# Seven products of quarter sums for the first expert matrix, weights fetched in four parts, tokens read back from DRAM

## The chip, the cores and the metric

The kernel runs on one core of a Trainium2 chip. The metric is the device time of one execution in microseconds (us). Five engines work side by side: TensorE (PE in the profile; PEld is its weight load), VectorE (DVE), ScalarE (ACT), GpSimd (POOL) and SyncE (SP), whose queue issues nearly all DMAs here.

## The reference

```python
attn_out = attention(q, k, v)             # 4 batches, 8 heads, 576 tokens, head 64, two sparse masks
x = attn_out as (2304, 512)
# first mixture, dense: every token goes through all 8 experts
P = exp(x @ w_gate - max), scaled 8 times by rows and by columns
out = 0
for e in range(8):
    h = np.maximum(x @ w1[e], 0.0)        # w1[e]: 512 x 1024
    ye = h @ w2[e]                        # w2[e]: 1024 x 512
    out += P[:, e:e + 1] * ye
# second mixture: each token goes to one expert, at most 288 tokens an expert
out2[mask] = relu(out[mask] @ w1b[e]) @ w2b[e]
```

## The kernel before

Every matrix is held as two f16 parts, a high one and a low one, and a product of two matrices is three f16 products (high·high, high·low, low·high) that accumulate in one PSUM bank. The span has three stages: attention, with expert 0 in blocks of 256 tokens beside it (to some 370 us); the other experts of the first mixture, one after another (to some 1640 us); and the routing and the experts of the second mixture.

Experts are counted from 0 here. Expert e of the first mixture works on blocks of 512 tokens (four, and one of 256). For one block `l1` (L729) makes 8 slices of 128 rows of h. A slice is 4 x 3 = 12 matmuls in one PSUM bank; ACT then writes the high part `hh` with its ReLU (L732), and DVE the low part `hl` (L733). `l2` (L747) makes the block's tiles of 128 tokens: 8 x 3 = 24 matmuls of 512 columns in a bank, which DVE adds, scaled, to the sum `acc` (L779, called done below). `blocks` issues l1 of block b+1 ahead of l2 of block b, so there are two sets of hh and hl, and TensorE always has a block whose inputs are ready. PSUM has 2 banks under the tag `bank`, 3 under `l1` and 3 under `l2`.

Work on weights runs beside this, in steps of a generator that `weave` spreads over the blocks by counts written out by hand, each step issued on its engine behind the last instruction of the block work (`behind`). `w_fetch` (L567) loads one raw f32 matrix of 2 MB into the one buffer `raw`; `w_scale` finds its largest value (four DVE reductions, L588, a POOL reduction over partitions, L594, and a few small DVE operations); `w_split` writes the high part on ACT (L612) and the low part on DVE (L616), four pieces of 1024 columns. `w_prep` does this for both matrices of the next expert, `m2_prep` for both matrices of an expert of the second mixture, whose parts go to DRAM (`wd`). `late_w` multiplies the last expert's second matrix by the second gate (128 DVE products of 256 columns, L929), and `logits` multiplies tokens by the second gate on DVE (L904).

All of these DMAs stand in SP's queue in the order in which a scheduler puts them, and an issue that waits for a buffer holds those behind it.

Of the kernel before, what the change touches and what calls it, by code (L numbers as in the profile page):

```python
# [39 lines left out]
EPAD = 3  # L40
# [21 lines left out]
DIRECT = 14, 15  # L62

# [28 lines left out]
class Kernel:  # L92
# [468 lines left out]

    def w_src(self, name, e, j):
        return self.a[f"{name}_w{j + 1}"][e].rearrange("(c p) f -> p c f", p=128)

    def w_fetch(self, name, e, j):
        r = self.ws_pool.tile([128, 4096], F32, name="raw").rearrange("p (c f) -> p c f", c=(DC, FC)[j])
        self.nc.sync.dma_start(out=r, in_=self.w_src(name, e, j))  # L567
        return r

    def loading(self):  # L570

        yield from self.pad(LOAD)

# [8 lines left out]
    def w_scale(self, r, j, inv, early):  # L582
# [12 lines left out]
        if early:  # L595
            yield
# [7 lines left out]
    def w_split(self, raw, s, hi, lo, mode="a"):  # L604
# [12 lines left out]
        else:  # L617
            nc.gpsimd.tensor_tensor(lo, raw, hi, op=OP.subtract)

# [7 lines left out]
    def w_prep(self, e, w, raw=None, js=(0, 1)):  # L627

        for j in js:
# [14 lines left out]
            for k in range(nw):  # L644
# [3 lines left out]
                yield  # L648

# [69 lines left out]
    def l1(self, w, t0, nb, h):  # L719

        nc = self.nc
        hh, hl = h
        for f in range(FC):
# [3 lines left out]
            for d in range(DC):  # L727
                for l, r in ((w[0], self.xh), (w[0], self.xl), (w[1], self.xh)):
                    nc.tensor.matmul(ps, l[:, d, fs], r[:, d, t0:t0 + nb], start=k == 0, stop=k == 3 * DC - 1)  # L729
                    k += 1  # L730
# [6 lines left out]
    def l2(self, w, t0, nb, h, done, fine=False):  # L737
# [3 lines left out]
        for j in range(nb // 128):  # L741
# [3 lines left out]
            for f in range(FC):  # L745
# [3 lines left out]
                if f < FC - 1 and (self.fine or fine and f % 2):  # L749
                    yield 0  # L750
            with self.tc.high_priority(offset=AHEAD):
# [10 lines left out]
            yield 2  # L762
# [30 lines left out]
    def blocks(self, jobs, pool, nb, fine=False):  # L793

        last = None
        for job in self.chain(jobs, (None,)):
            if job:
                e, w, t0, n, done = job
                h = [pool.tile([128, FC, nb], F16, name=x) for x in ("hh", "hl")]
# [45 lines left out]
    def m2_prep(self, e):  # L845

        nc = self.nc
        for j in range(2):
# [5 lines left out]
            for k in range(2):  # L854
# [3 lines left out]
                for p in (slice(0, 1024), slice(1024, 2048)):  # L858
                    self.w_split(rf[:, q][:, p], s, hi[:, p], lo[:, p])
                    yield  # L860
# [707 lines left out]
```

## Time and profile before

| what | value |
|---|---|
| time, median of 3 runs | 1994.17 us (1992.65 to 1994.55) |
| the profiled execution's own time | 2000.29 us |
| its span in the trace | 1998.4 us |
| TensorE busy | 1934.8 us, 97% |
| VectorE busy | 1159.3 us, 58% |
| ScalarE, GpSimd busy | 527.7 us (26%), 186.8 us (9%) |
| DMA | 172.05 MB, mean 86 GB/s |
| mean granted TensorE clock | 0.975 of full speed |

TensorE's busy time counts overlapping instructions once, so it shows how little of the span it stood without a matmul; how fast matmuls follow each other is read from the chain of work and the timeline.

### The profile page before, as it was taken

Reading aid. Unit: us, or ns where it says so; the run is one execution under the profiler, and the core shown is the slowest. Engines: PE = TensorE matmul, PEld = TensorE weight load, DVE = VectorE, ACT = ScalarE, POOL = GpSimd, SP = SyncE. Lnnn points to the kernel's source line nnn. Section 1 sums busy time; section 2 is a strip of 40 time slices with the busy share of each in tenths; the row PEclk is TensorE's granted clock in tenths of the full one; section 3 lists DMA queues with packets and bytes.
Section 4 is the critical chain, followed back from the end, with each engine's and each line's share of the span. In section 5 each row is a group of like instructions: output and inputs, shape, how many; then the busy total and the mean of one; then the engine's idle time right before and its main releaser. Section 6 shows DMA issues by size and latency. Waiting matters only on the chain.

```text
span 1998.4 us, 30818 instructions
## 1 busy us (share of the span) xinstructions
PE 1934.8 (97%) x12796; PEld 1101.8 (55%) x12796; DVE 1159.3 (58%) x2934; ACT 527.7 (26%) x1053; POOL 186.8 (9%) x272
## 2 busy tenths in 40 slices
PE   8899999999999999999999999999999999998997
PEld 7778777444544454454445444545454444666776
DVE  7687767465536554764555366434854788655530
ACT  4455543132123222111222133121201110222222
POOL 1423400000000000000000000000000002232231
PEclk9689999999999999999999999999999999998999
DMA  8412103014322441111134224321100003344360
GB/s 208 65 27 62 37 3 108 19 66 152 122 83 93 160 140 71 43 43 43 43 127 169 85 84 140 114 85 43 43 1 11 22 22 118 118 151 163 121 216 24
DMA packets 112252, 172.05 MB, mean 86 GB/s; under 512 B 65616, under 2 KB 70224, under 8 KB 107888
## 3 DMA queue, kind: packets, MB, share of 16 engines
q1 hardware_dynamic: 104432, 127.08, 19.7%
q0 software_dynamic: 7680, 43.01, 6.0%
q8 instruction: 100, 1.64, 0.3%
q14 instruction: 40, 0.33, 0.1%
HBM read 126.53 MB, written 43.54 MB: 85 GB/s over the span
## 4 chain that ended last, share of the span: by engine, by line
PE 75%; DVE 11%; DMA 6%; issue 4%; ACT 1%; POOL 1%; SPq 1%; another core or an unknown queue 0%; ACTq 0%; POOLq 0%; DVEq 0%
PE l L729 30%; PE l L747 30%; DMA raw<-in_moe_w_dram 5%; PE mm L1356 3%; PE mm L1384 3%; DVE wmx L588 3%; PE pcnt L1025 1%; DVE hl L733 1%; DVE m2l L616 1%; DVE w1l L616 1%; DVE w2l L616 1%; PE pt L282 1%; SPq L195 1%; PE ptp L414 1%; DMA wd<-m2l 1%
## 5 line engine op out<-in xcount | busy, mean ns | idle before, releaser
L729 PE MATMUL l<-xh,w1h 128*128 128x512 f16 (+1 forms) x1408 | 482.7, 343 | 12.7 <-DVE wmx L592 7.6
L729 PE MATMUL l<-xl,w1h 128*128 128x512 f16 (+1 forms) x1408 | 482.5, 343 | 0.0
L729 PE MATMUL l<-xh,w1l 128*128 128x512 f16 (+1 forms) x1408 | 482.4, 343 | 0.0
L747 PE MATMUL l<-w2h,hh 128*128 128x512 f16 x1152 | 437.7, 380 | 0.0
L747 PE MATMUL l<-w2l,hh 128*128 128x512 f16 x1152 | 437.2, 380 | 0.0
L747 PE MATMUL l<-w2h,hl 128*128 128x512 f16 x1152 | 437.2, 379 | 0.0
L729 PEld LDWEIGHTS <-w1h 128*128 128x128 f16 x2816 | 275.7, 99 | 241.2 <-issue 14.9
L732 ACT ACTIVATE hh<-l 128x512 f16<-128x512 f32 (+1 forms) x352 | 180.7, 517 | 765.8 <-PE l L729 765.3
L747 PEld LDWEIGHTS <-hh 128*128 128x128 f16 x2304 | 222.1, 98 | 258.3 <-issue 2.7
L733 DVE SCALAR_TENSOR_TENSOR hl<-l,hh 128x512 f16<-128x512 f32 (+1 forms) x352 | 206.4, 591 | 236.8 <-ACT hh L732 236.7
L779 DVE SCALAR_TENSOR_TENSOR acc<-l,pe,acc 128x512 f32<-128x512 f32 x126 | 94.2, 748 | 196.3 <-PE l L747 196.3
L729 PEld LDWEIGHTS <-w1l 128*128 128x128 f16 x1408 | 139.0, 99 | 112.8
L747 PEld LDWEIGHTS <-hl 128*128 128x128 f16 x1152 | 112.8, 98 | 136.3 <-issue 0.8
L588 DVE TENSOR_REDUCE wmx<-raw 128x1 f32<-128x1024 f32 x120 | 141.1, 1210 | 66.2 <-DMA raw<-in_moe_w_dram 66.2
L612 ACT ACTIVATE m2h<-raw,wscale 128x1024 f16<-128x1024 f32 x64 | 70.4, 1140 | 190.8 <-DVE iw L601 86.9
L616 DVE SCALAR_TENSOR_TENSOR m2l<-raw,wscale,m2h 128x1024 f16<-128x1024 f32 x64 | 80.1, 1281 | 46.0 <-DMA wd<-m2l 28.6
L594 POOL PARTITION_ALL_REDUCE wall<-wmx x32 | 11.2, 350 | 975.5 <-DVE wmx L592 975.5
L904 DVE SCALAR_TENSOR_TENSOR junk<-acc,raw 128x512 f32<-128x512 f32 x144 | 99.0, 688 | 3.4 <-DMA raw<-gt 1.5
L1361 DVE SCALAR_TENSOR_TENSOR h2l<-mm,h2h 128x288 f16<-128x288 f32 x64 | 28.6, 452 | 58.2 <-ACT h2h L1360 52.6
L929 DVE SCALAR_TENSOR_TENSOR junk<-raw 128x256 f32<-128x256 f32 x128 | 54.1, 423 | 11.7 <-DMA raw<-in_moe_w_dram 8.1
L612 ACT ACTIVATE w2h<-raw,wscale 128x1024 f16<-128x1024 f32 x28 | 30.1, 1137 | 93.0 <-DVE wscale L119 93.0
L325 ACT ACTIVATE sm<-sm,mx 72x72 f32<-72x72 f32 (+1 forms) x168 | 49.0, 371 | 1.3 <-DVE mx L317 1.1
(379 smaller groups left out, 2110.3 us busy)
## 6 DMA issues: line engine op xcount, KB each, us to landing
raw<-in_moe_w_dram SPq DMA_DIRECT2D x30, 2048.0 KB
wd<-m2h SPq DMA_DIRECT2D x32, 512.0 KB
wd<-m2l SPq DMA_DIRECT2D x32, 512.0 KB
q<-in_q_dram SPq DMA_DIRECT2D x32, 144.0 KB
k<-in_k_dram SPq DMA_DIRECT2D x32, 144.0 KB
acc<-in_moe_w_dram SPq DMA_DIRECT2D x2, 2048.0 KB
raw<-gt SPq DMA_DIRECT2D x2, 1024.0 KB
raw<-in_moe_w_dram SPq DMA_DIRECT2D x2, 1024.0 KB
```

Of the source, the lines that this page charges most:

```text
L588: nc.vector.tensor_reduce(mx[:, k:k + 1], r[:, k * n:k * n + n], axis=AX.XY, op=OP.max, apply_absolute_value=True)
L612: nc.scalar.activation(hi, raw, AF.Copy, scale=s1)
L616: nc.vector.scalar_tensor_tensor(lo, raw, s, hi, op0=OP.mult, op1=OP.subtract)
L729: nc.tensor.matmul(ps, l[:, d, fs], r[:, d, t0:t0 + nb], start=k == 0, stop=k == 3 * DC - 1)
L732: self.last = [nc.scalar.activation(hh[:, f, :nb], ps, AF.Relu).ins, nc.vector.scalar_tensor_tensor(hl[:, f, :nb], ps, 0.0, hh[:, f, :nb], ...
L733: nc.vector.scalar_tensor_tensor(hl[:, f, :nb], ps, 0.0, hh[:, f, :nb], op0=OP.max, op1=OP.subtract).ins]
L747: nc.tensor.matmul(ps, l[:, f, js], r[:, f], start=k == 0, stop=k == 3 * FC - 1)
L779: self.last = [nc.vector.scalar_tensor_tensor(a, ps, pe[:, c:c + 1], a, op0=OP.mult, op1=OP.add).ins]
L904: self.nc.vector.scalar_tensor_tensor(junk, self.acc[:, c], 1.0, self.wgb[:, e], op0=OP.mult, op1=OP.mult, accum_out=self.lg[:, c, e:e + 1])
L929: nc.vector.scalar_tensor_tensor(junk[:, :n], w[:, c], 1.0, g[:, e], op0=OP.mult, op1=OP.mult, accum_out=part[:, i, c, e:e + 1])
L1356: nc.tensor.matmul(ps, l[:, d, fs], xg[:, r], start=k == 0, stop=k == 3 * DC - 1)
L1384: nc.tensor.matmul(ps, l[:, f, dsl], r[:, f], start=k == 0, stop=k == 3 * FC - 1)
```

## The change

1. For experts 2 to 6 the first matrix and the tokens are cut in quarters, and the four quarters of h are made from seven products of sums of quarters in place of eight products. A block is 768 tokens (two halves of `PAIR` = 384), three blocks an expert. `group(g)` makes two slices of 128 rows of h (g and g+4) for the block: seven banks of 6 matmuls of 384 columns, which DVE, ACT and POOL add up in f32 in SBUF (`c1`, `c2`, `u2`, `m5`), and then ReLU and split on ACT and DVE. Four groups make a block's h; there is one set of hh and hl, in the space of the tokens `xh` and `xl`, and l2 of a block follows its groups at once.
2. The sums of quarters of the tokens are made in expert 1's stage (`x_sums`) and kept in DRAM (`xv`), beside a copy of the tokens (`xw`); each block loads its seven (393 KB each) into a ring of nine slots (`x_load`). The last expert reads tokens back from `xw` (`x_back`).
3. The sums of quarters of a first matrix (`w_sums1`) are made in the last l2 of the expert before.
4. A raw matrix is fetched by four DMAs, and split in pieces of 512 columns, with the low part one piece behind the high one (`splits`).
5. Expert 1 goes in blocks of 256 tokens. PSUM is 1 bank for `bank`, 5 for `l1` and 2 for `l2` until the last expert's end. `late_w` is made in two halves, in the stages of experts 1 and 3; half of the late logits move to expert 6's last block.

```diff
+LOAD2 = 14
...
-M2_AT = {1: (0, 1), 2: (2, 3), 3: (), 4: (4, 5), 5: (6, 7)}
+M2_AT = {2: (0, 1), 3: (2,), 4: (3, 4), 5: (5, 6), 6: (7,)}
+SIDE = {1: 24 + 27 + 46 + 19, 2: 170, 3: 140, 4: 170, 5: 170, 6: 130}
...
+PAIR = 384
+NBLK = N // (2 * PAIR)
+RING = 9
+
+W11, W12, W22, WS1, WS2, WS3, WS4 = range(7)
+X11, X21, X22, XT1, XT2, XT3, XT4 = range(7)
+PRODUCTS = (W11, X11), (WS2, XT2), (WS1, XT1), (WS3, XT3), (W12, X21), (WS4, X22), (W22, XT4)
+F_ORDER = [f + h * FC // 2 for f in range(FC // 2) for h in range(2)]
+BLOCK = 4 * 7 + 6 * 4
+HB = {"m5": 1, "u2": 1, "c1": 2, "c2": 1}
...
+    def x_sums(self, n, tiles):
+
+        nc = self.nc
+        g = nc.vector.tensor_tensor
+        a, b = (t[:, 0:PAIR] for t in tiles[:2])
+        outs = [t.bitcast(F16)[:, 0:2 * PAIR].rearrange("p (k t) -> p k t", k=2) for t in tiles[2:]]
+        t = n * 2 * PAIR
+
+        def out(v, c, s):
+            o = outs[v % 2]
+            nc.scalar.activation(o[:, 0], s, AF.Copy)
+            g(o[:, 1], s, o[:, 0], op=OP.subtract)
+            nc.sync.dma_start(out=self.xv[v, n, :, :, c], in_=o)
+        for c in range(2):
+            q = {k: (self.xh[:, d, t + o:t + o + PAIR], self.xl[:, d, t + o:t + o + PAIR])
+                 for k, d, o in ((11, c, 0), (12, c, PAIR), (21, c + 2, 0), (22, c + 2, PAIR))}
+            for v, l, r in ((XT1, 12, 11), (XT3, 22, 12)):
+                g(a, q[l][0], q[r][0], op=OP.subtract)
+                g(b, q[l][1], q[r][1], op=OP.subtract)
+                g(a, a, b, op=OP.add)
+                out(v, c, a)
+                yield
+                if v == XT1:
+                    g(b, q[22][0], a, op=OP.subtract)
+                    g(b, b, q[22][1], op=OP.add)
+                    out(XT2, c, b)
+                    yield
+                    g(a, b, q[21][0], op=OP.subtract)
+                    g(a, a, q[21][1], op=OP.subtract)
+                    out(XT4, c, a)
+                    yield
+
+    def x_load(self, n):
+
+        self.xb = {}
+        for _, v in PRODUCTS:
+            self.xb[v] = self.xr[self.xn % RING]
+            self.xn += 1
+            self.nc.sync.dma_start(out=self.xb[v], in_=self.xv[v, n])
...
+    def x_back(self, blocks):
+
+        for t, n in blocks:
+            for k, x in enumerate(self.xs.get(t, [x[:, :, t:t + n] for x in (self.xh, self.xl)])):
...
     def w_fetch(self, name, e, j):
-        r = self.ws_pool.tile([128, 4096], F32, name="raw").rearrange("p (c f) -> p c f", c=(DC, FC)[j])
-        self.nc.sync.dma_start(out=r, in_=self.w_src(name, e, j))
+
+        c = (DC, FC)[j]
+        r = self.raw.rearrange("p (c f) -> p c f", c=c)
+        src = self.w_src(name, e, j)
+        for k in range(0, c, c // 4):
+            self.nc.sync.dma_start(out=r[:, k:k + c // 4], in_=src[:, k:k + c // 4])
         return r
 
...
+    def splits(self, parts, s):
+
+        nc = self.nc
+        low = None
+        for raw, hi, lo in parts:
+            nc.scalar.activation(hi, raw, AF.Copy, scale=s)
+            if low:
+                nc.vector.scalar_tensor_tensor(low[2], low[0], s, low[1], op0=OP.mult, op1=OP.subtract)
+            low = raw, hi, lo
+            yield
+        nc.vector.scalar_tensor_tensor(low[2], low[0], s, low[1], op0=OP.mult, op1=OP.subtract)
...
+    def w_sums1(self):
+
+        nc = self.nc
+        g = nc.vector.tensor_tensor
+        H = FC // 2 * 128
+        r, s = self.wr, self.w1sc
+        n = H // 2
+        late = []
+        for k in range(2):
+            f = [slice(h * H + k * n, h * H + k * n + n) for h in range(2)]
+            a11, a12, a21, a22 = r[:, 0:2, f[0]], r[:, 2:4, f[0]], r[:, 0:2, f[1]], r[:, 2:4, f[1]]
+            t = self.wt[k]
+            o = slice(k * n, k * n + n)
+
+            def out(v, x, sc=s):
+                hi, lo = self.w1s[:, v, 0, :, o], self.w1s[:, v, 1, :, o]
+                nc.scalar.activation(hi, x, AF.Copy, scale=sc)
+                for l in late:
+                    nc.vector.scalar_tensor_tensor(*l, op0=OP.mult, op1=OP.subtract)
+                late[:] = [(lo, x, sc, hi)]
+            g(t, a21, a22, op=OP.add)
+            out(WS1, t)
+            yield
+            out(W11, a11)
+            g(a21, a11, a21, op=OP.subtract)
+            yield
+            out(WS3, a21)
+            g(t, t, a11, op=OP.subtract)
+            yield
+            out(WS2, t)
+            yield
+            out(W12, a12)
+            g(t, a12, t, op=OP.subtract)
+            yield
+            out(W22, a22, self.w1ns)
+            yield
+            out(WS4, t)
+            yield
+        for l in late:
+            nc.vector.scalar_tensor_tensor(*l, op0=OP.mult, op1=OP.subtract)
+        yield
...
+    def group(self, g):
+
+        nc = self.nc
+        hh, hl = self.hb
+        H = FC // 2
+        gs = slice(g * 128, g * 128 + 128)
+        a, b = slice(0, PAIR), slice(PAIR, 2 * PAIR)
+        tile = lambda name, n=1: self.hp.tile([128, n * PAIR], F32, name=name, bufs=HB[name])
+        v, add = nc.vector.tensor_tensor, nc.gpsimd.tensor_tensor
+        m5, u2, c1, c2 = tile("m5"), tile("u2"), tile("c1", 2), tile("c2", 2)
+
+        def split(f, c, t):
+            nc.scalar.activation(hh[:, f, t], c[:, t], AF.Relu)
+            todo.append(lambda: nc.vector.scalar_tensor_tensor(hl[:, f, t], c[:, t], 0.0, hh[:, f, t], op0=OP.max,
+                                                               op1=OP.subtract))
+        todo = []
+        for k, (w, x) in enumerate(PRODUCTS):
+            ps = self.bank("l1", "l1")[:, :PAIR]
+            n = 0
+            for c in range(2):
+                for l, r in ((0, 0), (0, 1), (1, 0)):
+                    nc.tensor.matmul(ps, self.w1s[:, w, l, c, gs], self.xb[x][:, r, c], start=n == 0, stop=n == 5)
+                    n += 1
+            now, todo = todo, []
+            with self.tc.high_priority(offset=AHEAD):
+                if k == 0:
+                    nc.scalar.activation(c1[:, a], ps, AF.Copy)
+                elif k == 1:
+                    v(u2, ps, c1[:, a], op=OP.add)
+                elif k == 2:
+                    nc.scalar.activation(m5, ps, AF.Copy)
+                    add(c1[:, b], u2, m5, op=OP.add)
+                elif k == 3:
+                    v(c2[:, a], ps, u2, op=OP.add)
+                    add(c2[:, b], c2[:, a], m5, op=OP.add)
+                elif k == 4:
+                    v(c1[:, a], ps, c1[:, a], op=OP.add)
+                    split(H + g, c2, b)
+                    split(g, c1, a)
+                elif k == 5:
+                    v(c1[:, b], ps, c1[:, b], op=OP.add)
+                    split(g, c1, b)
+                else:
+                    v(c2[:, a], ps, c2[:, a], op=OP.add)
+                    split(H + g, c2, a)
+                for f in now + (todo if k == 6 else []):
+                    self.last = [f().ins]
+            yield int(k in (0, 2))
+
+    def expert(self, e, order, first=None):
+
+        done = self.moe_done(e)
+        w2 = self.w2[e % 2]
+        for i, n in enumerate(order):
+            for g in range(FC // 2):
+                yield from self.group(g)
+            nxt = order[i + 1] if i + 1 < len(order) else first
+            if nxt is not None:
+                self.x_load(nxt)
+            else:
+                self.x_back(((2048, 256), (0, 512)))
+            yield from self.l2((None, None) + tuple(w2), n * 2 * PAIR, 2 * PAIR, self.hb, done, False,
+                               (3, 4, 5, 0, 1, 2))
...
+        self.banks = {"bank": 1, "l1": 5, "l2": 2}
...
+        for e in range(2, E - 1):
+            blk = self.expert(e, orders[e], orders[e + 1][0] if e + 2 < E else None)
+            side = [self.w_prep2(e + 1, self.w2[(e + 1) % 2])] + [self.m2_prep(k) for k in M2_AT[e]]
             if e == LATE_W:
-                side.append(self.late_w())
-                n += 65 + 2 * LOAD
-            self.weave((self.take(blk, 46 + 2 * (e > 1)), 55 if e == 1 else 58), (self.behind(self.chain(*side)), n))
-        self.weave((self.take(blk, 10), 10))
-        self.weave((self.take(blk, 24), 24), (self.behind(self.w_prep(E - 1, wts[1])), PIECES))
-        self.wgb = self.gate_bcast(self.ws_pool.tile([128, 4096], F32, name="raw"), 0, DM)
-        self.weave((self.take(blk, 22), 28), (self.behind(self.chain(*(self.logits(c) for c in LATE))), 4 * len(LATE)))
+                side.append(self.late_w(1))
+            if e == E - 2:
+                side.append(gates())
+            side.append(self.w_prep1(e + 1))
+            if e == E - 2:
+                side += [self.logits(c) for c in LATE[4:]]
+                for t, n, o in ((2048, 256, 0), (0, 512, 1024)):
+                    self.xs[t] = [x[:, o:o + DC * n].rearrange("p (d t) -> p d t", d=DC) for x in wf]
+            self.weave((self.take(blk, 2 * BLOCK + 4 * 7), 72), (self.behind(self.chain(*side)), SIDE[e]))
+            if e < E - 2:
+                self.weave((blk, 24), (self.behind(self.w_sums1()), 15))
+        fs = [slice(k, k + 512) for k in (0, 512)]
+        side = [self.splits([(self.wr[:, d, f], wts[1][0][:, d, f], wts[1][1][:, d, f]) for d in range(DC) for f in fs],
+                            self.w1sc)] + [self.logits(c) for c in LATE[:4]]
+        side = self.behind(self.chain(*side))
+        self.weave((blk, 24), (side, 20))
+        self.x_back(((t, 512) for t in (512, 1024, 1536)))
+        hs.close()
+        hb = hs.enter_context(tc.tile_pool(name="hb2", bufs=1, side="right"))
+        tail = w1s[:, 2 * DC * F:].rearrange("p (f t) -> p f t", t=512)
```

Three places of the order in which instructions stand.

VectorE in expert 3's stage before, in a block's l1 (`hl` is the low part of h, `m2l` that of a matrix of the second mixture):

```order
L601 TENSOR_TENSOR iw_66<-iw_66,wscale_i 128x1
L733 SCALAR_TENSOR_TENSOR hl<-l_7693,hh 128x512
L616 SCALAR_TENSOR_TENSOR m2l<-raw,wscale,m2h 128x1024 x2
L733 SCALAR_TENSOR_TENSOR hl<-l_7710,hh 128x512
L733 SCALAR_TENSOR_TENSOR hl<-l_7731,hh 128x512
L616 SCALAR_TENSOR_TENSOR m2l<-raw,wscale,m2h 128x1024
L733 SCALAR_TENSOR_TENSOR hl<-l_7748,hh 128x512
```

VectorE now, in the first group of expert 3's last block (`u`, `c`: sums of products in SBUF; `l`: PSUM banks; `xl`: the low part of h in its new place; `junk`: the products of `late_w`):

```order
L1027 TENSOR_TENSOR u_10393<-l_10412,c_10394 128x384
L1261 SCALAR_TENSOR_TENSOR junk,lwp<-raw 128x256 x3
L1032 TENSOR_TENSOR c_10395<-l_10437,u_10393 128x384
L1261 SCALAR_TENSOR_TENSOR junk,lwp<-raw 128x256 x2
L1035 TENSOR_TENSOR c_10394<-l_10446,c_10394 128x384
L1012 SCALAR_TENSOR_TENSOR xl<-c_10395,xh 128x384
L1039 TENSOR_TENSOR c_10394<-l_10456,c_10394 128x384
L1012 SCALAR_TENSOR_TENSOR xl<-c_10394,xh 128x384
L1042 TENSOR_TENSOR c_10395<-l_10467,c_10395 128x384
L1012 SCALAR_TENSOR_TENSOR xl<-c_10394,xh 128x384
L1261 SCALAR_TENSOR_TENSOR junk,lwp<-raw 128x256
L1012 SCALAR_TENSOR_TENSOR xl<-c_10395,xh 128x384
```

Where one operation per slice of h stood among the side work, a group of two slices has nine, five of which read a PSUM bank, and the side work stands between them.

SP's queue before, at the same expert (`raw` in parts of the first matrix, 128x4x1024, the second, 128x8x512, and `late_w`'s):

```order
L567 DMA raw<-in_moe_w_dram 128x4x1024
L567 DMA raw<-in_moe_w_dram 128x8x512
L912 DMA raw<-gt 128x8x256
L924 DMA raw<-in_moe_w_dram 128x8x256
L912 DMA raw<-gt 128x8x256
L924 DMA raw<-in_moe_w_dram 128x8x256
L567 DMA raw<-in_moe_w_dram 128x4x1024
```

SP's queue now, at the end of expert 3 (L632: sums of tokens into the ring, whose slots bear the names of the space they lie in; L753: raw, a first matrix as 128x1024, a second as 128x2x512):

```order
L1256 DMA raw<-in_moe_w_dram 128x8x256
L753 DMA raw<-in_moe_w_dram 128x1024
L632 DMA xr<-xv 128x1536
L632 DMA w1h<-xv 128x1536 x2
L632 DMA w1l<-xv 128x1536 x2
L632 DMA xh<-xv 128x1536 x2
L753 DMA raw<-in_moe_w_dram 128x1024 x3
L753 DMA raw<-in_moe_w_dram 128x2x512 x4
```

Three of the four parts of the next first matrix, and all of the second, now stand behind the seven loads of the next block.

## Rows read from the trace of the kernel before

**Rows 1.** The page: span, busy time by engine, chain that ended last by engine

```profile
span 1998.4 us, 30818 instructions
PE 1934.8 (97%) x12796; PEld 1101.8 (55%) x12796; DVE 1159.3 (58%) x2934; ACT 527.7 (26%) x1053; POOL 186.8 (9%) x272
...
PE 75%; DVE 11%; DMA 6%; issue 4%; ACT 1%; POOL 1%; SPq 1%; another core or an unknown queue 0%; ACTq 0%; POOLq 0%; DVEq 0%
```

**Rows 2.** Windows, all engines: start:end and length, then busy time by engine

```profile
0.00:100.00 100.00, 84.48 (x734) 71.57 (x735) 68.82 (x189) 49.15 (x142) 28.11 (x71) 0.81 0.64 137
...
500.00:600.00 100.00, 100.00 (x512) 49.98 (x511) 45.09 (x67) 21.18 (x32) 1.05 (x3) 1.00 0.27 101
...
1600.00:1700.00 100.00, 96.28 (x699) 45.56 (x698) 82.03 (x272) 10.31 (x16) 18.56 (x24) 0.98 0.20 72
...
380.00:800.00 420.00, 418.46 (x2034) 198.96 (x2033) 215.70 (x303) 106.36 (x145) 4.55 (x13) 1.00 0.30 106
800.00:1600.00 800.00, 797.06 (x3928) 384.21 (x3927) 451.32 (x977) 158.99 (x236) 10.45 (x25) 1.00 0.19 68
```

**Rows 3.** Chain in order of time, expert 2: start, length, engine, line, count

```profile
497.53 20.72 PE l L747 x96
518.25 10.48 PE l L729 x96
...
549.45 20.72 PE l L729 x96
```

**Rows 4.** Lines of PE, shapes apart: count, busy us, mean ns, idle before

```profile
L729 PE MATMUL l<-xh,w1h 128*128 128x512 f16 x896 | 339.6, 379 | 4.2 <-DVE hl L733 2.8 <-DVE wmx L592 1.4
L729 PE MATMUL l<-xh,w1h 128*128 128x256 f16 x512 | 143.1, 279 | 8.5 <-DVE wmx L592 6.2 <-DVE hl L733 1.8 <-DVE p L683 0.4
```

**Rows 5.** Lines of DVE, shapes apart

```profile
L904 DVE SCALAR_TENSOR_TENSOR junk<-acc,raw 128x512 f32<-128x512 f32 x144 | 99.0, 688 | 3.4 <-DMA raw<-gt 1.5
L779 DVE SCALAR_TENSOR_TENSOR acc<-l,pe,acc 128x512 f32<-128x512 f32 x126 | 94.2, 748 | 196.3 <-PE l L747 196.3
L616 DVE SCALAR_TENSOR_TENSOR m2l<-raw,wscale,m2h 128x1024 f16<-128x1024 f32 x64 | 80.1, 1281 | 46.0 <-DMA wd<-m2l 28.6 <-ACT m2h L612 17.4
L929 DVE SCALAR_TENSOR_TENSOR junk<-raw 128x256 f32<-128x256 f32 x128 | 54.1, 423 | 11.7 <-DMA raw<-in_moe_w_dram 8.1
...
L929 DVE DVE_READ_ACCUMULATOR junk<-raw 128x1 f32 x128 | 10.5, 82 | 0.0
...
L253 DVE SCALAR_TENSOR_TENSOR kq<-pt,kq 128x384 f16<-128x384 f32 x18 | 9.1, 552 | 5.7 <-ACT kq L252 5.5
```

**Rows 6.** Timeline of DVE and POOL, 66 to 81.5 us: start, length

```profile
67.37 0.92 POOL L245 TENSOR_TENSOR vo<-hl,vh 128x384 f16<-128x384 f32 x1
67.45 2.05 DVE L616 SCALAR_TENSOR_TENSOR w1l<-acc,wscale,w1h 128x512 f16<-128x512 f32 x2
...
78.18 1.56 POOL L244 TENSOR_SCALAR hh<-hh,vscale 72x512 f32<-72x512 f32 x1 [3.80 <-ACT vh L242]
78.73 1.41 DVE L616 SCALAR_TENSOR_TENSOR w1l<-acc,wscale,w1h 128x512 f16<-128x512 f32 x2
...
80.06 1.48 DVE L253 SCALAR_TENSOR_TENSOR kq<-pt,kq 128x384 f16<-128x384 f32 x3
```

**Rows 7.** Lines of ACT and of POOL, shapes apart

```profile
L252 ACT ACTIVATE kq<-pt 128x384 f16<-128x384 f32 x18 | 7.6, 487 | 2.7 <-PE pt L282 2.4
...
L245 POOL TENSOR_TENSOR vo<-vl,vh 128x384 f16<-128x384 f32 x8 | 7.1, 888 | 0.7
```

**Rows 8.** Chain, its DMAs and reductions: start, length

```profile
422.24 9.46 DMA raw<-in_moe_w_dram
431.72 3.47 DVE wmx L588 x3
...
1024.34 3.03 DMA wd<-m2l
```

**Rows 9.** Waits: SP's longest sum, and DVE's for ACT, 380 to 1600 us

```profile
SPq L567 <- DVE w1l L616: 294.7, 7, 69.8
...
DVE hl L733 <- ACT hh L732: 208.6, 153, 2.5
```

More of the change, by code (lines that the diff above doesn't have):

```diff
@@ L739, in l2 @@
+    def l2(self, w, t0, nb, h, done, fine=False, tiles=None):
         nc = self.nc
         hh, hl = h
-        for j in range(nb // 128):
+        for j in tiles or range(nb // 128):
             ps = self.bank("l2", "l2")
@@ L744, in l2 @@
             k = 0
-            for f in range(FC):
+            for f in F_ORDER if tiles else range(FC):
                 for l, r in ((hh, w[2]), (hh, w[3]), (hl, w[2])):
@@ L1409, in layers @@
         self.gt = dram.tile([E, DM], F32, name="gt")
+        self.xv = dram.tile([7, NBLK, 128, 2, 2, PAIR], F16, name="xv")
+        self.xw = [dram.tile([128, DC, N], F16, name=f"xw{k}") for k in range(2)]
+        self.xs = {}
+        self.load = LOAD
         st = ExitStack()
@@ L1457, in layers @@
         self.route_consts()
+        wts[1] = self.w_views([w1s[:, 0:DC * F], w1s[:, DC * F:2 * DC * F]]) + self.w2[1]
         self.weave((self.sinkhorn(), 10), (self.w_prep(1, wts[1]), PIECES), (self.take(blk, 100, True), 48))
[L1459 to L1462 removed]
@@ new lines, in layers @@
+        temps = [v for n in ("m2h", "m2l") for t in [self.m2.tile([128, 2048], F16, name=n).bitcast(F32)]
+                 for v in (t[:, 0:512], t[:, 512:])]
+        for n in range(NBLK):
+            self.x_store(n)
+        for c in range(DC):
+            nc.sync.dma_start(out=self.gt.rearrange("e (c p) -> p c e", p=128)[:, c], in_=self.wg2[:, c])
+        for k, x in enumerate((self.xh, self.xl)):
+            nc.sync.dma_start(out=self.xw[k], in_=x)
+        side = [self.x_sums(n, temps) for n in range(NBLK)] + [self.w_prep2(2, self.w2[0])]
@@ new lines, in layers @@
+        side += [self.late_w(0), self.w_prep1(2)]
+        self.load = LOAD2
+        self.weave((self.take(blk, 86), 28), (self.behind(self.chain(*side)), SIDE[1]))
+        self.weave((blk, 8), (self.behind(self.w_sums1()), 15))
+        hs.close()
+        self.hp = hs.enter_context(tc.tile_pool(name="hb", bufs=1, side="right"))
+        ring.append(self.hp.tile([128, nx], F16, name="xr"))
+        self.xr = [r.rearrange("p (k c t) -> p k c t", k=2, c=2) for r in ring]
+        self.xn = 0
+        orders = [list(range(NBLK)) for _ in range(E)]
@@ new lines, in layers @@
+        tail = w1s[:, 2 * DC * F:].rearrange("p (f t) -> p f t", t=512)
+        h2 = [[tail[:, 0:FC], Two(tail[:, FC:], hb.tile([128, FC // 2, 512], F16, name="hx"))],
+              [hb.tile([128, FC, 512], F16, name=n) for n in ("hh", "hl")]]
+        blk = self.blocks(self.jobs(E - 1, wts, 512), None, 512, False, h2)
+        self.weave((self.take(blk, 12), 12), (side, 6))
+        self.drain(side)
+        g = self.gate_bcast(self.raw, 0, DM)
+        self.wgb = [g[:, 2 * k:2 * k + 2] for k in range(4)]
```

243 lines of the change are left out of this document (193 added, 50 removed).

## The prediction

> **What bounds the kernel now.** I read the page first: TensorE is busy 97% of 1998.4 us, VectorE 58%, and 75% of the chain that ended last is TensorE's [rows 1]. A busy share hides which stage has slack, so I read the windows next. Between 380 and 1600 us TensorE lacks 1.5 + 2.9 = 4.5 us (420 - 418.46, 800 - 797.06), while VectorE works 51% and 56% of the time [rows 2]. Before and behind this stretch TensorE has holes (84.48 of the first 100 us, 96.28 of 1600 to 1700). So experts 1 to 7 run at the pace of TensorE's matmuls alone, and fewer of them there save time nearly one for one, as long as nothing new is late.
>
> The pace is in the chain [rows 3]: 96 matmuls of 512 columns take 20.72 us, 0.2158 us each; 96 of 256 take 10.48 us, 0.1092 us each. The mean "379 ns" and "279 ns" [rows 4] are lengths of overlapping matmuls and are not the pace; the groups are used for their counts. The two points lie almost on a line through zero, so 384 columns should cost (0.2158 + 0.1092)/2 = 0.1625 us. No 384-wide expert matmul stands in the trace; its bounds are 3/4 of a 512 (0.1619) and 3/2 of a 256 (0.1638).
>
> **What the change removes on TensorE.** Before, the first matrix of one expert is 4 blocks x 20.72 + 10.48 = 93.4 us. Now it is 3 blocks x 4 groups x 42 matmuls = 504 of 384 columns: 504 x 0.1625 = 81.9 us. That is 11.5 us an expert, **-57.4 us** for five; by the bounds of the pace -59 to -54. The second matrix keeps its 432 matmuls. Expert 1 in blocks of 256 takes 9 x 10.48 = 94.3 instead of 93.4: **+0.9 us**. Of the 4.5 us of holes some go with the new order; I take **-1 us**.
>
> **What it adds on VectorE.** A group lasts 42 x 0.1625 = 6.8 us on TensorE. It gives VectorE nine operations of 128x384, five of which free a bank. The nearest row is a 384-wide operation from PSUM at 552 ns [rows 5]; three in a row took 1.48 us [rows 6], so (1.48 - 0.55)/2 = 0.465 us from start to start. Nine are 4.2 us, at full durations 5.0. ACT's six at 487 ns are 2.9 us and POOL's two at 888 ns 1.8 us [rows 7]: neither fills 6.8 us. Where before VectorE waited for ACT's ReLU (208.6 us, 153 times) [rows 9], that now is a chain bank, ACT copy, VectorE sum, and so on; five banks under `l1` cover it: TensorE can run about four products, 4 x 6 x 0.1625 = 3.9 us, ahead of the evacuation. In l2 two banks let done lag by one tile, 24 x 0.2158 = 5.2 us.
>
> Side work comes on top. An expert's splits are pieces of 512 columns, 0.67 us in a pair (1.41 us for two) [rows 6]; reductions are 1.16 us each (3.47 for three) [rows 8]. For an expert beside which two experts of the second mixture are prepared: five matrices, each 4 reductions and 8 pieces, 5 x (4.6 + 5.4) = 50; the first matrix's reductions 4.6; its 22 operations of sums at 0.67, 14.7; together about 69 us. Groups take 12 x 4.2 = 50 and 18 dones at 0.75 us [rows 5] 13.5. That is 133 of 175 us (81.9 + 93.2), 76%. Over an expert VectorE keeps up; the question is bursts within a group.
>
> In most groups some 2 us of side work fit: 4.2 + 2 = 6.2 of 6.8. Two places are heavier. In the last block of expert 3 the order shows 7 products of `late_w` in the first group; at 0.42 + 0.08 us [rows 5] they are 3.5 us. 4.2 + 3.5 = 7.7, and with 0.7 us lost to POOL (below) 8.4: 1.6 us late a group, 6.4 in four, of which 3.9 are covered: **+2.5 us**. In expert 6's last block 4 to 5 logits a group at 0.69 us [rows 5] plus 0.08 make the same: 4.5 x 0.77 = 3.5; **+2.5 us**. Bounds: 0 if other dips absorb them, 6 us each if nothing is covered.
>
> A pair of splits started beside a two-input POOL operation took 2.05 us, against 1.41 for a pair beside a one-input POOL operation [rows 6]; 0.64 us were lost once. A group now has two two-input POOL adds, so I take 0.7 us a group, bounds 0 and 2 x 0.89 = 1.8 [rows 7].
>
> **Loads.** Each block loads 7 x 393 KB = 2.75 MB. A raw matrix of 2.1 MB landed in 9.46 us [rows 8], 222 GB/s; at that pace 2.75 MB are 12.4 us. They are issued as slots of the ring come free in the last group, and l2 then lasts 6 x 24 x 0.2158 = 31.1 us: hidden, unless other transfers double it. The copies, stores and sums of tokens in experts 0 and 1 stand off TensorE's path: sums are 84 operations at 0.465 = 39 us of VectorE in a stage of 187 us. The stores of tokens are queued on SP among attention's q, k and v loads, where a hold would reach TensorE; I take +1 us, bounds 0 and 6.
>
> **Expert switches.** The sums of the next first matrix must be ready when l2 ends. At expert 3's end three raw parts stand behind seven loads of tokens, some 12.4 us, then 3/4 of 9.46, 7 us, a last reduction and the scale, 2 us, and half of the 22 operations, 7.4 us: 29 of 31.1. The second half of the sums is wanted two groups (13.6 us) later. It just fits; at the other switches the raw matrix comes earlier. SP's longest waits were already of this kind, 294.7 us for a buffer that splits had to free [rows 9], and hidden. I take **+2.5 us** for five switches, bounds 0 and 5 x 8. The last expert's tokens come back before it starts: first blocks before the last l2, the rest one block of 41 us (2 x 20.72) later; nothing.
>
> Raw in four parts lets reductions start at the first part; the reductions are hidden now, so nothing.
>
> **Sum.** -57.4 + 0.9 - 1 + 2.5 + 2.5 + 1 + 2.5 = -49.0 us. Against the profiled execution's own 2000.29 us (1.9 us more than its span) that is 1951.3. The median is 0.3% below that execution, 1994.17/2000.29; so 1951.3 becomes **1945 us**.
>
> **Rivals.**
>
> A. VectorE and POOL block each other in every group. For it: the 2.05 us pair. Against: the 1.41 us pair beside POOL. If both adds are paid in full, a group is 4.2 + 1.8 + 2 = 8.0 us, 1.2 late, 4.8 a block, 0.9 beyond the cover; with 3 us of side work 2.2 late, 8.8 a block, 4.9 beyond. With about half of the 15 blocks of either kind it is 7 x 0.9 + 8 x 4.9 = 45 us at worst; half of that, as VectorE often reads only one SBUF operand beside the add, is 22: some **1965 us**. [...]
>
> B. Switches wait: the sums are 8 us late at each of five switches, 40 us back: **1985 us**, because loads share the DMA engines with raw parts. For it: the 29 of 31.1 us. Against: one switch only has that order.
>
> C. Slower: VectorE's operations in a group take far longer than 0.465 us. It decides from the point where four groups are late by the cover plus a block's share of the gain, 3.9 + 57.4/15 = 7.7 us, 1.9 a group: 8.75 us, or (8.75 - 2)/9 = 0.75 us an operation. At twice 0.465, 0.93, a group is 10.4 us: 3.6 late, 14.4 a block, 10.5 beyond the cover, 15 blocks 157 us, less 49: **2102 us**. For it: waits between ACT, VectorE and POOL within one group. Against: 552 ns is the full length of one.
>
> D. Matmuls of 384 keep the pace of 512 (0.2158): 504 x 0.2158 = 108.8 us, 15.4 more an expert, 77 in all, slower too. The 256-wide pace excludes all but a trace of it.
>
> **Chances.** Forecast (1933 to 1957) 0.68; A 0.15; B and the like 0.08; C 0.07; D 0.02. The range runs from 1933 (every stall hidden: 57.4 + 1 + 3 below) to 1968, past A: it leaves out B, C, D and a few hundredths below. About 0.2%, 4 us, is what a measurement can tell here from no change. B, near 1985, is still faster; a part of B and C ends within 4 us. Faster 0.90, same 0.03, slower 0.07.
>
> **What would show it.** Right: in experts 2 to 6 the chain has TensorE runs of 42 matmuls in 6.8 us; an expert lasts 175 us; TensorE's holes there sum to under 15 us, at expert 3's and 6's last blocks. Wrong by A or C: TensorE idle in groups, released by VectorE's bank readers, and 384-wide operations above 0.6 us beside POOL's adds. Wrong by B: TensorE idle at the first group of an expert, released by ACT's or VectorE's sums. Wrong in the main term: the pace of 384-wide matmuls away from 0.1625 us.

## The result, and the profile after

The changed kernel takes 2015.49 us (2014.02 to 2016.47), against 1994.36 us before: ratio 1.0105, 95% interval 1.0088 to 1.0121. It is slower by 21 us where 49 us less were forecast. The profiled execution took 2015.86 us.

The page after (span, busy time by engine; answers to [rows 1]):

```profile
span 2014.1 us, 33864 instructions
PE 1893.1 (94%) x13300; PEld 1149.9 (57%) x13300; DVE 1416.6 (70%) x3590; ACT 642.6 (32%) x1411; POOL 314.7 (16%) x392
```

TensorE's busy time fell by 41.7 us while the span grew by 15.7: the matmuls were saved and the time went into waiting. The stage of experts 2 to 6, from the first matmul of a group to the last of l2, in one window (columns as in [rows 2]):

```profile
560.40:1508.40 948.00, 893.58 (x4680) 458.53 (x4679) 717.20 (x1391) 315.28 (x594) 136.13 (x147) 0.99 0.43 143
```

Forecast for it were 5 x 175.0 = 875 us. It took 948: 54.4 us in which TensorE stood (948.00 - 893.58), and 18.6 more busy time than the matmuls need. What ended TensorE's waits there (us in all, times, longest):

```profile
PE l L1020 <- DVE u L1027: 19.2, 8, 4.1
PE l L1020 <- ACT c L1025: 11.9, 7, 3.3
PE l L1020 <- DVE c L1039: 8.4, 8, 2.0
```

The groups (L1020) wait for those who empty their banks: for VectorE's first operation, for ScalarE's first copy, and for L1039, which needs a GpSimd add. So the next views are what held VectorE and GpSimd. VectorE's own waits in that stage:

```profile
DVE m2l L812 <- DMA wd<-m2l: 49.3, 10, 5.9
DVE xl L1012 <- ACT xh L1011: 37.9, 42, 1.6
DVE wscale_i L142 <- POOL wall L780: 32.6, 25, 3.6
DVE wmx L774 <- DMA raw<-in_moe_w_dram: 22.1, 22, 2.5
...
DVE c L1039 <- POOL c L1030: 14.3, 6, 3.8
...
DVE junk L1261 <- DMA raw<-in_moe_w_dram: 5.8, 1, 5.8
```

Side work waits for DMAs at the head of VectorE's queue (first and fourth row), and both side work and groups wait for GpSimd (third, fifth). Before, the waits for stores and for all-reduces were (380 to 1600 us):

```profile
DVE m2l L616 <- DMA wd<-m2l: 28.6, 16, 2.5
DVE wscale_i L117 <- POOL wall L594: 15.7, 28, 0.8
```

Both are longer now, the longest 5.9 us in place of 2.5 and 3.6 in place of 0.8.

One group in expert 4's stage, on GpSimd (start, length, idle before and releaser):

```profile
1009.73 1.00 POOL L1033 TENSOR_TENSOR c<-c,m 128x384 f32<-128x384 f32 x1
1016.71 0.38 POOL L780 PARTITION_ALL_REDUCE wall<-wmx  x1 [5.98 <-DVE c L1032]
1024.61 0.98 POOL L1030 TENSOR_TENSOR c<-u,m 128x384 f32<-128x384 f32 x1 [7.53 <-issue]
```

and on VectorE:

```profile
1014.10 0.55 DVE L1027 TENSOR_TENSOR u<-l,c 128x384 f32<-128x384 f32 x1
...
1017.12 0.15 DVE L142 TENSOR_SCALAR wscale_i<-wall 128x1 f32<-128x1 f32 x1 [1.35 <-POOL wall L780]
...
1025.62 0.56 DVE L1039 TENSOR_TENSOR c<-l,c 128x384 f32<-128x384 f32 x1 [3.76 <-POOL c L1030]
```

and TensorE, at both ends of that stretch:

```profile
1008.67 2.08 PE L1020 MATMUL l<-w1h,w1s 128*128 128x384 f16 x6 [3.33 <-DVE u L1027]
1010.54 2.68 PE L1020 MATMUL l<-xh,w1s 128*128 128x384 f16 x12
1013.05 2.11 PE L1020 MATMUL l<-xl,w1s 128*128 128x384 f16 x12
...
1015.98 2.11 PE L1020 MATMUL l<-w1h,w1s 128*128 128x384 f16 x12
...
1026.24 1.14 PE L1020 MATMUL l<-xr,w1s 128*128 128x384 f16 x6 [2.02 <-DVE c L1039]
```

GpSimd's add at 1024.61 (L1030) needed a sum that VectorE had started at 1014.10, yet GpSimd stood 7.53 us behind its all-reduce, with nothing to wait for that the profile shows ("issue"). L1039 waited for the add, and TensorE for L1039's bank. In the lines of L780 and L1030 the trace has this record (count, ns, first and last start):

```profile
L780 POOLq MODIFY_POOL_CONFIG  x32: 6/12/18, 588.7 to 1410.2; - x32
...
L1030 POOLq MODIFY_POOL_CONFIG  x36: 82/83/83, 536.5 to 1444.5; - x36
```

The all-reduce's line of the kernel before has none. In GpSimd's order of instructions the changed kernel has 16 such places ahead of an all-reduce and 18 ahead of an add, printed as an instruction without operands:

```
L780 ISA
L780 ISA wall_8230<-wmx2_8228 128x1
L1030 ISA
L1030 TENSOR_TENSOR c1_8319<-u2_8318,m5_8317 128x384
```

A place has two of the records, 32 and 36 in all; one more change stands ahead of another all-reduce (L1272, at 909 us). So there are 35 changes from adds to all-reduces or back. In the twelve before which the profile shows nothing to wait for ("issue"), GpSimd stood 5.8 to 7.5 us (7.53 us above); most of the others lie in longer waits for inputs, where what a change takes can't be seen.

### The profile page after: what moved, and what is told of

It reads as the page before. It is cut to its first block, busy times and chain, and to the rows that moved or that the text cites. A ratio compares the mean times of both kernels' runs of the same rounds, so it can differ in the third digit from the quotient of the medians.

```text
span 2014.1 us, 33864 instructions
## 1 busy us (share of the span) xinstructions
PE 1893.1 (94%) x13300; PEld 1149.9 (57%) x13300; DVE 1416.6 (70%) x3590; ACT 642.6 (32%) x1411; POOL 314.7 (16%) x392
## 5 line engine op out<-in xcount | busy, mean ns | idle before, releaser
L1020 PEld LDWEIGHTS <-w1s 128*128 128x128 f16 x2520 | 248.6, 99 | 222.1 <-issue 62.9
L1073 PE MATMUL l<-w2h,xh 128*128 128x512 f16 x720 | 272.9, 379 | 7.3 <-DVE acc L1107 3.8
L1073 PE MATMUL l<-w2h,xl 128*128 128x512 f16 x720 | 272.5, 379 | 2.6 <-DVE xl L1012 2.4
L1073 PE MATMUL l<-w2l,xh 128*128 128x512 f16 x720 | 272.9, 379 | 0.0
L1073 PEld LDWEIGHTS <-xh 128*128 128x128 f16 x1440 | 140.4, 98 | 177.0 <-issue 6.1
L991 PEld LDWEIGHTS <-w1s 128*128 128x128 f16 x1344 | 131.5, 98 | 62.7 <-issue 4.8
L774 DVE TENSOR_REDUCE wmx<-raw 128x1 f32<-128x1024 f32 x120 | 143.4, 1212 | 25.9 <-DMA raw<-in_moe_w_dram 25.8
L1012 DVE SCALAR_TENSOR_TENSOR xl<-c,xh 128x384 f16<-128x384 f32 x240 | 131.3, 558 | 42.6 <-ACT xh L1011 37.9
L991 PE MATMUL l<-xh,w1s 128*128 128x256 f16 (+1 forms) x768 | 154.3, 299 | 3.8 <-DVE hl L995 3.6
L1030 POOL TENSOR_TENSOR c<-u,m 128x384 f32<-128x384 f32 x60 | 63.8, 1064 | 480.1 <-DVE u L1027 264.1
L1073 PE MATMUL l<-w2h,hh 128*128 128x512 f16 x352 | 134.6, 382 | 0.0
L1073 PE MATMUL l<-w2l,hh 128*128 128x512 f16 x352 | 134.4, 382 | 0.0
L1073 PE MATMUL l<-w2h,hl 128*128 128x512 f16 x352 | 134.2, 381 | 0.0
L1020 PE MATMUL l<-w1h,w1s 128*128 128x384 f16 x576 | 105.8, 329 | 15.3 <-ACT c L1025 9.0
L1020 PE MATMUL l<-xh,w1s 128*128 128x384 f16 x576 | 105.8, 331 | 14.6 <-DVE u L1027 14.1
```

Source lines behind the costliest of these rows:

```text
L774: nc.vector.tensor_reduce(mx[:, k:k + 1], r[:, k * n:k * n + n], axis=AX.XY, op=OP.max, apply_absolute_value=True)
L991: nc.tensor.matmul(ps, l[:, d, fs], r[:, d], start=k == 0, stop=k == 3 * DC - 1)
L1012: todo.append(lambda: nc.vector.scalar_tensor_tensor(hl[:, f, t], c[:, t], 0.0, hh[:, f, t], op0=OP.max, op1=OP.subtract))
L1020: nc.tensor.matmul(ps, self.w1s[:, w, l, c, gs], self.xb[x][:, r, c], start=n == 0, stop=n == 5)
L1030: add(c1[:, b], u2, m5, op=OP.add)
L1073: nc.tensor.matmul(ps, l[:, f, js], r[:, f], start=k == 0, stop=k == 3 * FC - 1)
```

## Experiments

Theory W: VectorE's and ScalarE's queues are held by side operations that wait for DMAs. Rivals: L (the loads of tokens make those DMAs late), T or S (too much or too dense work for VectorE), G (waits within a group), and P, formed after the first two sets (GpSimd's changes between adds and all-reduces). Ratios are to the kernel before on the same chip; a difference between two of these kernels is taken from their ratios, times 1994 us.

**e1, loads of tokens once:** `x_load` issues only while `self.xn <= RING`.

> Leaves out all loads of sums of tokens but the first nine, so blocks multiply old sums; all arithmetic stays. Theory W (side operations that wait for a DMA at the head of VectorE's and ScalarE's queues hold the evacuations of the groups; the DMAs are the raw parts and the stores of m2h and m2l, whatever the loads of tokens do): stores and raw parts still take their 2 to 10 us, so only a small part comes back, 2000 to 2010 us. Rival L (the 41 MB of loads, by their share of the DMA engines or their place ahead of the stores in SP's queue, make those DMAs late): the stalls go, 1945 to 1960 us. Rival T (VectorE has simply too much work in the groups): no change, 2015 us.

2005.43 us, 1.0061 (1.0033 to 1.0089): 9 us, by the ratio, of the 70 between forecast and result. VectorE's waits for stores stay at 49.9 us. L is a small part.

**e2, stores that nothing waits for, e3, no raw fetches either, e4, no preparation at all:**

```diff
-                nc.sync.dma_start(out=self.wd[2 * j][e * 128:e * 128 + 128, q], in_=hi)
+                nc.sync.dma_start(out=self.wd[2 * j][e * 128:e * 128 + 128, q], in_=x[0])   # x: self.xw
-            r = self.w_fetch("moe2", e, j)                                                  # e3
+            r = self.raw.rearrange("p (c f) -> p c f", c=(DC, FC)[j])
```

> The stores of the second mixture's parts are replaced by copies of the same size from DRAM to DRAM, so that nothing waits for m2h and m2l to be free (the stored values are not the weights). Theory W: 49 us of VectorE's and 27 us of ScalarE's waits for these stores go; about half of the stalls of TensorE, 1975 to 1990 us. Rival L: 2000 to 2015 us, since the traffic stays. Rival T: 2015 us.

> As the run with copies in place of stores, and the raw matrices of the second mixture are not fetched: their reductions and splits read what the buffer holds, so VectorE and ScalarE do the same work and wait for none of these DMAs. Theory W: most stalls go, 1945 to 1965 us. Rival L: 1960 to 1990, as less traffic is left. Rival T: 2005 to 2015 us, since the work is all there.

> Leaves out all preparation of the second mixture's weights in the stages of experts 2 to 6 (about 40 us of VectorE per expert; copies from DRAM to DRAM fill their place). Theory W and rival T both: the stalls go, 1940 to 1955 us; if the time stays above 1980 the cause is in the groups themselves (waits between ScalarE, VectorE and GpSimd, rival G).

2007.44 (1.0079, 1.0051 to 1.0106), 2003.87 (1.0046, 1.0028 to 1.0064) and 1962.48 us (0.9851, 0.9828 to 0.9874). The copies ran early, beside expert 1, filled the DMA engines there (share 0.91 to 0.98 from 300 to 460 us in e3) and put off the first group from 560 to 579-581 us in all three. Their times are therefore some 19 us too high, and two were made anew with stores from tiles that exist later (the repeats came out 18 and 21 us lower by the ratios):

**e5 and e6, as e3 and e4, stores from `w1s` and the new second matrix:**

> All arithmetic of the side work, none of its DMA waits for the second mixture: its raw matrices are not fetched, and the stores to DRAM read other tiles of the same size that are ready at the stage's start (the stored values are not the weights). The earlier run of this kind let copies run in expert 1's stage and cost 18 us there; this one doesn't. Theory W (waits for DMAs at the head of VectorE's queue): 1950 to 1965 us. Theory S (the side work itself comes in runs that VectorE can't do beside the groups): 1980 to 1990 us, some 30 us below the changed kernel and 35 above one without the work.

> Leaves out the preparation of the second mixture's weights in the stages of experts 2 to 6, with stores of other tiles in its place, none of them in expert 1's stage. Theories W and S: 1940 to 1948 us, the groups at the pace of TensorE. Rival G (waits within a group): above 1960 us.

1986.27 us (0.9954, 0.9934 to 0.9973) and 1946.19 us (0.9748, 0.9723 to 0.9772). Without the preparation the forecast holds, so G falls. In e6 23 of the 35 changes are left, and TensorE waits 4.2 us in the whole stage: where this side work is absent, a change costs little. Without the DMA waits of the preparation, those for stores and those for raw parts together, 30 us come back and 41 stay (against e6). I took that for S; the next set spoke against it, but for two blocks (see e12).

**e7, halves of the buffers:** a split of 1024 columns and its store alternate between two halves of `m2h` and `m2l`.

```diff
-            for k in range(2):
-                q = slice(k * 2048, k * 2048 + 2048)
+            for k in range(4):
+                q = slice(k * 1024, k * 1024 + 1024)
+                b = k % 2 * 1024
```

> Computes what the changed kernel does; the parts for DRAM are made and stored in halves of the two buffers, so that a split waits only for the store before the last. Theory W: 49 us of waits for stores shrink to under 10 and some 25 us come back, 1985 to 1995 us. Theory S: 5 to 12 us come back, 2003 to 2010, as the same runs of work are late elsewhere.

2034.68 us, 1.021 (1.0173 to 1.0246): slower, against both theories. Twice as many stores stand in SP's queue, where they wait for their splits and hold what is behind: SP's waits for ScalarE's parts went from 123.0 to 200.0 us and for VectorE's from 33.5 to 103.5, VectorE's for raw parts from 22.1 to 33.6; VectorE's waits for stores fell only from 49.3 to 34.8. That this is the cause was not tried.

**e8, less side work in groups:** `yield int(k == 0)` in `group`, 60 in place of 72 in the weave.

> Computes what the changed kernel does; a group counts one step and not two when side work is spread, so groups get about half of the side work they had, and the tiles of l2 more. Theory S: VectorE's lateness in groups falls, but tiles of l2 (5.2 us each, with up to 8 us of side work in a run) get later: 2005 to 2020 us, the place of the stalls moves from groups to l2. If groups alone were the trouble: 1990 to 2000 us. Theory W: no change, 2013 to 2017 us.

2012.48 us, 1.0077 (1.0049 to 1.0105): 6 us by the ratios, and the intervals overlap. Where the steps stand matters little.

**e9, each partition's own maximum (in the scaling of weights from expert 1's stage on), e10, adds on VectorE:**

```diff
-        nc.gpsimd.partition_all_reduce(al, m2, channels=128, reduce_op=bass_isa.ReduceOp.max)   # e9
+        al = m2
-        v, add = nc.vector.tensor_tensor, nc.gpsimd.tensor_tensor                               # e10
+        v, add = nc.vector.tensor_tensor, nc.vector.tensor_tensor
```

> Leaves out GpSimd's all-reduce over partitions in the scaling of weights from expert 1's stage on (each partition's own maximum stands for it, so the scales are not the reference's); all DMAs and all of VectorE's work stay. Theory P (GpSimd stands still for 6 to 7 us each time it goes from its adds to an all-reduce or back, and VectorE, which waits for either, holds the groups' banks): most stalls go, 1950 to 1970 us. Theory S (VectorE's runs of side work are too dense): 2005 to 2015 us. Theory W: 2005 to 2015 us, the waits for stores and raw parts stay.

> Computes what the changed kernel does; the two adds of each group go from GpSimd to VectorE, 120 operations of 0.47 us, 56 us more for it; GpSimd has only its all-reduces. Theory P: faster in spite of the added work, 1960 to 1990 us. Theory S: slower, 2030 to 2070 us. Theory W: 2015 to 2030 us.

1986.42 us (0.9955, 0.9939 to 0.9971) and 1977.85 us (0.9908, 0.9872 to 0.9944). Both end GpSimd's changes, one by taking the all-reduces, one by taking the adds; by their records 2 are left in e9's stage and none in e10's. Although VectorE's busy time grows by 38.5 us (1416.6 to 1455.1 over the span; 56 were expected), e10 is 39 us faster than the changed kernel, and faster than the kernel before: S falls as the main cause, P holds. Its stage in one window, TensorE's longest wait in it, and VectorE's waits for stores and for all-reduces:

```profile
560.40:1470.50 910.10, 888.25 (x4686) 460.02 (x4685) 752.86 (x1504) 318.63 (x595) 11.78 (x27) 0.99 0.44 149
```

```profile
PE l L1020 <- ACT c L1025: 8.8, 5, 3.3
...
DVE m2l L812 <- DMA wd<-m2l: 52.5, 10, 7.0
...
DVE wscale_i L142 <- POOL wall L780: 7.0, 16, 0.6
```

The waits for stores stay as they were; the longest wait for an all-reduce fell from 3.6 to 0.6 us.

**e11, the maximum by way of DRAM:** 128 values are stored, read back to all partitions and reduced on VectorE.

> Computes what the changed kernel does; in place of GpSimd's all-reduce the 128 maxima go to DRAM and come back to all partitions by two DMAs, and VectorE reduces 128 values, five steps later. Theory P: 1955 to 1985 us, faster than the kernel before. Theories S and W: 2010 to 2030 us.

2235.45 us, 1.1195 (1.1154 to 1.1235): a miss. VectorE waited for the values that come back:

```profile
DVE wall L788 <- DMA junk<-mxd: 220.9, 23, 12.8
```

The values that two small DMAs in a row bring back are waited for up to 12.8 us at the head of VectorE's queue; that is W once more, and larger. SP's queue is held too until the first of the two has landed: 22 waits from 560 to 1508 us, 155.3 us in all, up to 8.3.

**e12, both parts gone** (e10 and e5):

> The adds on VectorE, and none of the second mixture's DMA waits (its raw matrices are not fetched, the stores read other tiles, so the stored values are not the weights); VectorE's work is all there, 56 us more than in the changed kernel. If switches of GpSimd and waits for DMAs are the whole cause: 1945 to 1958 us. If dense runs of work (theory S) hold a part: 1965 to 1980 us.

1947.27 us, 0.9761 (0.9732 to 0.9791). Its stage:

```profile
568.00:1444.90 876.90, 876.15 (x4679) 457.63 (x4678) 754.15 (x1503) 320.58 (x594) 11.98 (x27) 1.00 0.33 115
```

TensorE lacks 0.75 us in 876.90, with VectorE busy 754 us (86%). With the adds on VectorE and without the DMA waits nothing of the loss is left. But moving the adds did more than end the changes, as two blocks show. In expert 3's last block, with `late_w`, the four groups took 36.4 us from the first of these matmuls to the second, where e12 takes 27.6:

```profile
870.03 1.14 PE L1020 MATMUL l<-xr,w1s 128*128 128x384 f16 x6
...
906.46 0.38 PE L1073 MATMUL l<-w2h,xh 128*128 128x512 f16 x1
```

No change of GpSimd stands there (none between 847 and 909 us). VectorE works almost without a pause (34.9 of the 36.4 us), and its products take longer beside an add:

```profile
888.29 0.41 DVE L1261 SCALAR_TENSOR_TENSOR junk<-raw 128x256 f32<-128x256 f32 x1
...
888.74 1.09 DVE L1261 SCALAR_TENSOR_TENSOR junk<-raw 128x256 f32<-128x256 f32 x1
```

```profile
888.51 1.04 POOL L1030 TENSOR_TENSOR c<-u,m 128x384 f32<-128x384 f32 x1 [4.86 <-DVE u L1027]
```

In expert 6's last block, with the logits, they took 34.9 us, where e12 takes 27.3. In e9, almost without changes, the two are still 34.8 and 34.6 us; in e10 they are 31.2 and 29.2. These 9 us are about what e10 is ahead of e9. Whether the longer operations beside adds cost them was not tried apart: the order of instructions in e10 also has less side work there (16 products between the first and the fourth group's start, against 22).

**e13, other places for empty steps, e14, and a third bank for l2** (both on e10):

```diff
-                for _ in range(STORE):
+                for _ in range(0 if k else 3 * STORE):          # and LOAD2 = 12
-        self.banks = {"bank": 1, "l1": 5, "l2": 2}
+        self.banks = {"l1": 5, "l2": 3}                         # e14
```

> Computes what the changed kernel does: the adds on VectorE, six empty steps of side work behind the first store of a matrix's halves (two before) and none behind the second, and 12 instead of 14 behind a fetch, so that the number of steps is the same. If the waits for stores at the head of VectorE's queue are what is left: 1958 to 1970 us. If not: 1974 to 1982 us as with the adds alone.

> As the run with moved empty steps, and l2 has three PSUM banks instead of two (the one that no other work of the stage uses). If VectorE is late by more than one tile at the end of an l2: 5 to 10 us below that run; if its lateness shows only in the groups: the same within 3 us.

1982.32 us (0.9944, 0.9927 to 0.9962) and 1985.07 us (0.9936, 0.9913 to 0.996; single runs from 1970 to 1991). Neither helps: the waits for stores are still 47.4 us in e13 (52.5 in e10), so the moved empty steps gave the stores hardly any time.

**e15, stores that nothing waits for, e16, loads of tokens once, e17, no raw fetches** (each on e10):

> The adds on VectorE; the stores of the second mixture's parts read other tiles of the same size (the stored values are not the weights), so no split waits for a store; the raw matrices are fetched. If the waits for stores are the rest of the loss: 1948 to 1958 us. If raw parts are: 1970 to 1978 us.

> The adds on VectorE; leaves out all loads of sums of tokens but the first nine, so blocks multiply old sums. If these loads make the stores and raw parts late: 1950 to 1960 us. If not, as with the adds alone: 1970 to 1980 us.

> The adds on VectorE; the raw matrices of the second mixture are not fetched (what the buffer holds is split), the stores stay. If raw parts, by their landing or by the DMA engines that they fill, are the rest of the loss: 1948 to 1958 us. If the waits for stores are, whatever is fetched: 1968 to 1978 us.

1942.78 us (0.9747, 0.9714 to 0.978), 1970.04 us (0.9881, 0.9849 to 0.9913) and 1953.84 us (0.9791, 0.9745 to 0.9837). With free stores the whole second part comes back, 32 us. This takes away two things that were not tried apart: VectorE's waits for the stores, and SP's waits for the parts that it stores (for ScalarE's 127.6 us in e10), which hold the raw fetches behind them; VectorE's waits for raw parts fell with them from 20.5 to 8.6 us. Without raw fetches (e17) VectorE's waits for stores fall to 29.1 us and 23 us come back: raw fetches, which e15 keeps, cost little by their own landing and more by what they do to the stores. The loads of tokens give 5 us by the ratios, which is not clear of noise: the intervals of e10 and e16 overlap.

## Why the prediction was wrong

- **The main term** was right. Twelve 384-wide matmuls start 1.95 us apart in the trace (1015.98 to 1017.93 on TensorE), 0.1625 us each as forecast, and where next to nothing waits (e12, e15, e6) the time is 1943 to 1947 us against 1945. What the sum missed is in the stage of the groups, 948 us against 875, and there in the stalls and what they bring with them.
- **"ACT's six ... POOL's two ... neither fills 6.8 us"** is the step that failed first. GpSimd was priced by the lengths of its adds. What it does between them was not: the order printed operand-less instructions ahead of all-reduces and adds, and I passed over them. Where it shows, each change is 5.8 to 7.5 us, about a whole group. With the changes gone 30 us come back (e9), or 39 (e10, which alters more than that).
- **The burst sum (+2.5, +2.5 us)** counted side work as work only. A split's wait for the store of the buffer it writes was in [rows 5], 28.6 us at L616, and cost next to nothing before (TensorE lacked 4.5 us from 380 to 1600 us). Now it is 49.3 us, its longest 5.9 in place of 2.5, and five bank readers a group stand behind it in the same queue; which of the two made it dear was not tried. Without it 30 us come back (e5, with the waits for raw parts) or, from e10 on, 32 us (e15). The two places that the term names were also under-priced: their four groups took 9 and 8 us longer than 27.3, not 2.5 each. A group's 8.4 us came true in the first (VectorE's first operations stand at 879.49 and 887.82); the 3.9 us of cover did not, as VectorE came late there, after a wait of 5.8 us for `late_w`'s raw part. Elsewhere the amount of side work was harmless: with the adds on it as well VectorE kept pace (e12).
- **The switch term (+2.5 us) and rival B:** at the first group of each of the five experts TensorE did not wait; its longest wait of all, 4.1 us, stood in the first group of expert 3's last block. B did not happen.
- **Rival A** was priced at 20 us and is part of the truth; means hide it. The operation on L1012 takes 558 ns over all, against 552 with the adds gone, because only 6 of 240 ran beside an add: these took 778 on average, up to 1026, the others 552. Of the splits (L812) 14 ran beside an add, with 1074 ns on average and up to 1486, where 747 is their length alone. In all VectorE's operations lost some 14 us beside adds. An add took 981 ns alone and up to 1449 beside such an operation, where 888 was the row [rows 7]. VectorE's operations that read a PSUM bank kept their 550 ns beside an add: 110 of them took 552 on average, 541 to 559. The 23 reductions (L774), which read one operand in SBUF, took 1210 ns beside an add and 1211 alone. The 22 us halved the full price because VectorE often reads only one SBUF operand beside the add; no row was given for that, it was an estimate, and these two groups are what the run showed of it. What the longer operations cost in time stays open: about the 9 us between e9 and e10 at most.
- **Rival C** had the sign and 0.07. Its point of decision, 0.75 us an operation, was not reached by the operations of the groups: 0.55 us long, but for those beside adds. Waiting, which its "for it" names, did what length was to do.

## What to carry to other kernels

What an operation cost here was its length, what the engine did to get to it (5.8 to 7.5 us where a change of GpSimd showed), and what it waited for while others stood behind it in the engine's queue (up to 5.9 us for a store). Before moving work that TensorE waits for onto an engine, list all that already waits in that queue, also the waits that cost nothing so far. On GpSimd, look for operand-less instructions in the order before all-reduces and elementwise operations are mixed in a tight stage (here 34 of them, and 30 us in e9). To see whether two engines hinder each other, take the operations that ran side by side, and not a mean over all (778 ns on L1012, where the mean was 558). Here the version with the adds on VectorE (1977.85 us, 0.9908) beats both kernels. Another 32 us stand behind its stores (e15); a way to keep the stores and not to wait for them was tried once, from the changed kernel (e7), and was slower.

## What the runs showed of the hardware

The clock made some long stalls dearer. After TensorE had worked 1.34 of 4 us the granted clock was 0.57 in the next window (columns as in [rows 2]; the last number pair is DMA share and GB/s, the clock stands ahead of it):

```profile
1004.00:1008.00 4.00, 1.34 (x9) 0.69 (x7) 3.92 (x4) 0.00 (x0) 0.00 (x0) 1.00 0.97 325
1008.00:1012.00 4.00, 3.33 (x12) 1.61 (x12) 3.69 (x7) 1.24 (x3) 1.95 (x2) 0.57 0.22 84
```

The six matmuls from 1008.67 to 1010.54 took 1.87 us, 0.31 each, where they start 0.1625 apart at a granted clock of 1.00; the twelve behind them took 2.51 us (to 1013.05) in place of 1.95. So this stall of 3.33 us cost 1.5 us on top. Not every stall did this: after the one of 3.69 us at 1201.34 and the one of 2.02 us at 1026.24 six took 0.97 us and the clock stayed at 1.00, no loss. Over the stage the granted clock was 0.991, the mean of windows of 4 us: by that, an estimate, 948 x 0.009 = 8.5 us went to the lower clock, about half of the stage's 18.6 us of extra busy time (893.58 less 875). The other 10 us, an estimate too, are stall that the record counts as busy: a matmul is recorded 0.33 us long (1.14 us for six that start 0.1625 apart), 0.16 beyond the next one's start, and stands so ahead of each of some 60 waits. In e12, without stalls, 876.15 us are busy and the mean clock is 1.00.
